# Lightning attention and a bilinear FFN on one core: the first FFN step of four token groups as seven block products

## The chip, the cores and the metric

The kernel runs on one core of a Trainium2 chip. The metric is the device time of one execution in microseconds (us). A core has five engines with queues of their own: TensorE (PE; its weight loads are listed apart as PEld), VectorE (DVE), ScalarE (ACT), GpSimd (POOL) and SyncE (SP), which here issues nearly all DMAs. Each engine takes its instructions in the order in which the program gives them, so an instruction that waits holds up all that stands behind it on that engine.

## What is computed

Attention with decay in blocks, then a bilinear FFN, all in float32 outside and bf16 inside the matrix products:

```
q, k, v: (4, 8, 768, 64)      # batch, heads, sequence, head size
for each block of the sequence:
    intra = ((qb @ kb.T) * Dmask) @ vb
    inter = (qb * lam_pow) @ kv_state
    out   = intra + inter
    kv_state = lam_block * kv_state + (kb * rev_pow).T @ vb

x = out as (3072 tokens, 512)
a = x @ w_a                   # 512 x 1536
b = x @ w_b                   # 512 x 1536
y = (a * b) @ w_out           # 1536 x 512
```

The result y is 3072 x 512 in float32.

## The kernel before

The tokens are cut into 24 units of 128 (a unit is 128 positions of one batch entry, all heads). `GROUPS` = (4, 1, 2, 4, 4, 4, 4, 1) joins units into eight groups; group 3 holds units 7 to 10, group 4 holds 11 to 14, and so on, and the last group is unit 23 alone. The FFN of a group runs while the attention of units further on is worked in between its matmuls. Group 0 also brings in the weights: they come as float32 through the 12 staging buffers of `wst_pool` and are cast to bf16 into `wa_sb`, `wb_sb` and `wo_sb`.

The FFN of a later group (`ffn`, L518) has two stages. In the first, each of 12 column blocks f of the weights takes four matmuls for `a_ps` and four for `b_ps` (`half`, L465): weights 128x128 stand still, up to 512 tokens of xT move. ScalarE copies `a_ps` to `a_sb` (L477), VectorE multiplies `a_sb` with `b_ps` into `ab` (L495). In the second, the output stage, each unit t of the group takes 12 matmuls into `op` (L515), ScalarE copies the result to `o_sb` (L510), and SP stores it. The outputs of the first three groups are kept in `wst` buffers (L505) and stored in group 3.

What is done between the matmuls is written out by hand in `PLAN`: for each group a list of (slot, piece, unit). `hook(slot)` issues the pieces of a slot; slots 0 to 11 follow the column blocks f, slots 12 and up the half units of the output stage (12 + 2t after the first six matmuls of unit t, 13 + 2t after its store). In group 0 slots 12 to 35 follow pairs of output matmuls. The pieces:

- P (also split into PK and PV): `prep_k` (L298) multiplies k and q by powers of lam (L276; POOL, for units 4 and 5 k on VectorE), from unit 7 on issues a DMA transpose on SP (L304) to make `qkT`; `prep_v` (L309) casts v to `vb` (L295; POOL up to unit 6, then VectorE) and calls `pump` (L188), which issues the loads of units further on. How far on is set by `LOOKAHEAD`: three units while fewer than nine are prepared, then two, with exceptions at 9 and 10. The loads have four buffers per tensor.
- T: transposes on PE for units 4 to 6 (L318), with a copy by ScalarE (L320).
- S: scores on PE (L332) and their masks on VectorE (L349). V: the state update on PE (L396) and its copy on VectorE (L429). O, O2, Q: `pieces_O` (L442): inter and intra matmuls (L366), ScalarE's copies to xT (L389), and in Q the scores and masks of two more units before and after.
- C: a cast of `wo_sb`. W: a store of a kept output.

PSUM has seven banks of this kernel in rotation (`ps_bank`, L110), which a piece can hold, and one for the state. An allocation takes the next bank that is not held; the first writer of the new tile waits for the last reader of the old one.

Of the kernel before, what the change touches and what calls it, by code (L numbers as in the profile page):

```python
# [16 lines left out]
F32 = mybir.dt.float32  # L17
BF16 = mybir.dt.bfloat16
# [4 lines left out]
def _bc(ap, dims):  # L23
# [4 lines left out]
GROUPS = (4, 1, 2, 4, 4, 4, 4, 1)  # L28
# [11 lines left out]

PLAN = {
    0: [(0, "V", 3), (8, "C", 0), (9, "C", 1), (15, "C", 2), (18, "C", 3), (23, "PK", 4),
        (26, "C", 4), (26, "T", 4), (29, "C", 5), (29, "S", 4), (30, "PV", 4), (33, "O", 4),
# [4 lines left out]
        (9, "S", 7), (9, "S", 8), (6, "PK", 10), (10, "V", 8), (11, "PV", 10),  # L50
        (12, "Q", (7, 8, 9, 10)), (12, "P", 11), (13, "V", 9), (14, "P", 12),
        (14, "O2", (9, 10))],
    3: [(6, "S", 11), (6, "S", 12)],
}
for _g, _u in ((3, 11), (4, 15), (5, 19)):
    PLAN.setdefault(_g, []).extend(
        [(1, "P", _u + 2), (3, "P", _u + 3), (6 if _g == 3 else 4, "V", _u),
         (9 if _g == 3 else 7, "Q", (_u, _u + 1, _u + 2, _u + 3)), (10, "P", _u + 4),
         (12, "P", _u + 5), (13, "V", _u + 2), (16, "Q", (_u + 2, _u + 3, _u + 4, _u + 5))])
PLAN[3] += [(_s, "W", None) for _s in range(12, 19)]  # L60
PLAN[5] = [(_s, _n, (21, 22, 23) if _us == (21, 22, 23, 24) else _us)
           for _s, _n, _us in PLAN[5] if _us != 24]
PLAN[6] = [(4, "O", 23)]


@with_exitstack
def kernel(
# [11 lines left out]
    nc = tc.nc  # L79
    B, H, S, D = q.shape  # L80
# [3 lines left out]
    d_model, d_ff = moe_w_a.shape  # L84
# [4 lines left out]
    FC = d_ff // 128  # L89
# [3 lines left out]
    wst_pool = ctx.enter_context(tc.tile_pool(name="wst", bufs=W_BUFS))  # L93
    ld_pool = ctx.enter_context(tc.tile_pool(name="ld", bufs=4))
# [3 lines left out]
    xT_pool = ctx.enter_context(tc.tile_pool(name="xT", bufs=2))  # L98
    a_pool = ctx.enter_context(tc.tile_pool(name="a", bufs=5))
    ab_pool = ctx.enter_context(tc.tile_pool(name="ab", bufs=2))  # L100
    o_pool = ctx.enter_context(tc.tile_pool(name="o", bufs=4))
    ps_pool = ctx.enter_context(tc.tile_pool(name="ps", bufs=1, space=PSUM))
    kvps_pool = ctx.enter_context(tc.tile_pool(name="kvps", bufs=1, space=PSUM))

# [5 lines left out]
    def ps_bank(name, shape, dt, hold=False, ffn=False, at=None):  # L110
        i = bank["next"] if at is None else at
        while i in bank["held"] or (ffn and i == bank["ffn"]):
            i = (i + 1) % 7
        if ffn:
            bank["ffn"] = i
        bank["next"] = (i + 1) % 7
        if hold:
            bank["held"].add(i)
        return ps_pool.tile(shape, dt, name=name, tag=f"ps{i}")
# [6 lines left out]

    def load_x(w, u):
        b, nb = divmod(u, NB)
        t = ld_pool.tile([128, H, D], F32, name=w + "f", tag=w + "f")
        nc.sync.dma_start(out=t, in_={"q": qr, "k": kr, "v": vr}[w][b, nb])  # L130
        raw[u, w] = t

# [176 lines left out]
    def prep_v(u):  # L309
        make_vb(u, "pool" if u < n0 + 3 else "dve")  # L310
        pump()
# [70 lines left out]
    def evac_o(us, b, eng="act"):  # L382
        xT, col = xTs[us[0]]
        n = len(us)
        o = U[us[0]]["o"][b]
        src = _bc(o, [o.ap[0], [2 * BLK, 2], [1, n * BLK]])
        dst = xT[:, 2 * b:2 * b + 2, col:col + n * BLK]
        if eng == "act":
            nc.scalar.copy(dst, src)  # L389
        else:  # L390
            nc.vector.tensor_copy(dst, src)
# [48 lines left out]
    xTs = {}  # L440

    def pieces_O(us, nxt=()):  # L442
        kqs = [score_banks() for u in nxt]
        o_banks(us)
        for u, kq in zip(nxt, kqs):
            scores(u, kq)
        for u in us:
            inter(u)
        for b in range(2):
            for u in us:  # L450
                intra(u, b)
            evac_o(us, b)
        beside = len(us) == 2 and us[0] >= n0 + 5
        if beside:
            kv_beside(us[1])
        for u, kq in zip(nxt, kqs):
            masks(u, kq)
        if beside and us[1] % NB < NB - 1:
            kv_copy(us[1], kv["ps"])
# [34 lines left out]
        ps = half(wb_sb, f, xT, "b_ps", 0, gt)  # L494
        nc.vector.tensor_mul(ab[:, f, :gt], a_sb[:, :gt], ps[:, :gt])  # L495

    kept = []

    def store_kept():
        row, o_sb = kept.pop(0)  # L500
# [1 line left out]

    def store(row, op, lo, hi, queue=None):
        if row < g_u0[KEEP_GROUPS]:
            o_sb = wst_pool.tile([128, 1024], F32, name="o_kept", tag="wst")[:, :d_model]  # L505
            nc.scalar.copy(o_sb, op)
            kept.append((row, o_sb))
            return
        o_sb = o_pool.tile([128, d_model], F32, name="o_sb", tag="osb")
        nc.scalar.copy(o_sb[:, lo:hi], op[:, lo:hi])  # L510
        (queue or nc.sync).dma_start(out=out_r[row][:, lo:hi], in_=o_sb[:, lo:hi])

    def out_mms(op, ab, t, fs, lo=0, hi=d_model):
        for f in fs:
            nc.tensor.matmul(op[:, lo:hi], lhsT=ab[:, f, t * 128:(t + 1) * 128],  # L515
                             rhs=wo_sb[:, f, lo:hi], start=(f == 0), stop=(f == FC - 1))

    def ffn(u0, n, xT, hook, first, last):  # L518
        gt = n * BLK
        ab = ab_pool.tile([128, FC, 512], BF16, name="ab", tag="ab")  # L520
        if first:
            for i, cs in enumerate(W_STEPS):
                nxt = W_STEPS[i + 1] if i + 1 < len(W_STEPS) else ()
                fs = range(w_off[cs[0]] // 128, w_off[cs[-1] + 1] // 128)
                a_sbs = a_parts(fs[:2], xT, gt) if i == 0 else []
                a_sbs += [a_part(f, xT, gt) for f in fs[len(a_sbs):]]
                if i == 0:
                    cast_w("b", cs[1], "act")
                else:
                    for c in nxt:  # L530
                        cast_w("a", c, "dve")
                for n_f, (f, a_sb) in enumerate(zip(fs, a_sbs)):
                    b_part(f, xT, gt, a_sb, ab)
                    hook(f)
                    if i == 0 and n_f == 1:
                        cast_w("a", nxt[0], "dve")
                for c in nxt:
                    cast_w("b", c, "act")
            ops = [ps_bank("op", [128, d_model], F32, hold=True) for _ in range(n)]
            slot = FC  # L540
            for c in range(FC // 2):
                for t in range(n):
                    out_mms(ops[t], ab, t, range(2 * c, 2 * c + 2))
                    if c == FC // 2 - 1:
                        store(u0 + t, ops[t], 0, d_model)
                    hook(slot)
                    slot += 1
            bank["held"].clear()
            return
        for f in range(FC):  # L550
            a_sb = a_part(f, xT, gt)
            b_part(f, xT, gt, a_sb, ab)
            hook(f)
        for t in range(n):
            op = ps_bank("op", [128, d_model], F32, ffn=True)
            if last and t == n - 1:
                for lo, hi in ((0, 256), (256, 384), (384, 512)):
                    if lo:
                        op = ps_bank("op", [128, d_model], F32, ffn=True)
                    out_mms(op, ab, t, range(FC), lo, hi)  # L560
                    store(u0 + t, op, lo, hi, nc.scalar if hi == d_model else None)
                return
            out_mms(op, ab, t, range(FC // 2))
            hook(FC + 2 * t)
            out_mms(op, ab, t, range(FC // 2, FC))
            store(u0 + t, op, 0, d_model)
            hook(FC + 2 * t + 1)


    gx = {}  # L570
# [134 lines left out]
    for g, n in enumerate(GROUPS):  # L705
        if g + 1 < len(GROUPS):
            new_xT(g + 1)
        plan = {}
        for slot, name, us in PLAN.get(g, ()):
            plan.setdefault(slot, []).append((name, us))  # L710

        def hook(slot, plan=plan):
            for name, us in plan.get(slot, ()):
                if name == "C":
                    cast_w("o", us, "dve")
                elif name == "PK":
                    prep_k(us)
                elif name == "PV":
                    prep_v(us)
                elif name == "P":  # L720
                    prep_k(us)
                    prep_v(us)
                elif name == "W":
                    store_kept()
                elif name == "T":
                    piece_T(us)
                elif name == "S":
                    piece_S(us)
# [12 lines left out]
_INS = ['q', 'k', 'v', 'lam', 'moe_w_a', 'moe_w_b', 'moe_w_out']  # L741
# [26 lines left out]
```

## Time and profile before

Three runs gave 231.8, 232.08 and 233.04 us, median 232.08. The profiled execution spans 230.2 us from the first to the last instruction, at a granted TensorE clock of 0.999. By group, each row the busy time in a stretch of that execution:

| stretch, us | what | PE | DVE | ACT | POOL | DMA, GB/s |
|---|---|---|---|---|---|---|
| 51.3 to 62.2 | group 1 | 10.85 | 6.11 | 6.48 | 6.86 | 197 |
| 62.2 to 82.3 | group 2 | 19.73 | 14.45 | 7.68 | 8.17 | 197 |
| 82.3 to 117.5 | group 3 | 34.79 | 20.93 | 11.52 | 12.62 | 235 |
| 117.5 to 152.1 | group 4 | 34.39 | 17.37 | 11.51 | 8.53 | 165 |
| 152.1 to 187.0 | group 5 | 34.58 | 16.05 | 11.51 | 2.22 | 76 |
| 187.0 to 218.8 | group 6 | 31.64 | 8.26 | 10.02 | 0.00 | 34 |

A row of a group listing reads: line, engine, operation, output and input tiles, shapes and number; after the first bar the busy time in all (us) and the mean of one (ns); after the second the idle time of the engine just ahead of these instructions and what ended it. A row of a timeline reads: start, length (us), engine, line, operation, tiles, number of instructions merged, and in brackets the idle time before it. On PE the end of a matmul is modelled, so consecutive ones overlap in the print; the distance between starts is what counts.

### The profile page before, as it was taken

What the parts mean: (1) busy time and instruction counts of PE and PEld (TensorE: products, weight loads), DVE (VectorE), ACT (ScalarE), POOL (GpSimd) and SP (SyncE); (2) the same over time, 40 slices, a digit from 0 to 9 for tenths busy, and PEclk for the clock granted to TensorE, in tenths of its full rate; (3) what the DMA queues carried; (4) which work ended last, traced back from release to release, by engine and by line L of the source; (5) the groups of instructions that cost most, each with busy time, mean ns of one, the idle gap of its engine ahead of it and who ended that gap; (6) DMA issues with size and microseconds to landing.
All of it is one profiled execution on the core that took longest, in us unless ns stands there. A gap on an engine that the chain in (4) does not pass through costs nothing.

```text
span 230.2 us, 4630 instructions
## 1 busy us (share of the span) xinstructions
PE 221.4 (96%) x1816; PEld 121.0 (53%) x1839; DVE 118.2 (51%) x205; ACT 88.8 (39%) x172; POOL 49.9 (22%) x65
## 2 busy tenths in 40 slices
PE   7699999999999999999999999999999999999994
PEld 2475444459688544454544454544454544444493
DVE  0994865736488845876416574426574313341050
ACT  2686563056433243242233342233342233432261
POOL 6061000228351436333302433002100000000000
PEclk9999999999999999999999999999999999999999
DMA  4999999999999999999979995249200220000211
GB/s 130 317 277 347 363 387 293 303 217 196 202 211 182 215 186 231 233 195 200 350 222 217 157 235 89 94 116 205 48 0 0 94 91 0 4 0 31 106 48 47
DMA packets 97542, 39.37 MB, mean 171 GB/s; under 512 B 85488, under 2 KB 92016, under 8 KB 97520
## 3 DMA queue, kind: packets, MB, share of 16 engines
q1 hardware_dynamic: 97232, 39.00, 75.2%
q8 instruction: 14, 0.23, 0.4%
q10 hardware_dynamic: 288, 0.07, 0.1%
q14 instruction: 8, 0.07, 0.1%
HBM read 28.32 MB, written 6.29 MB: 150 GB/s over the span
## 4 chain that ended last, share of the span: by engine, by line
PE 92%; DMA 3%; SPq 1%; issue 1%; ACT 1%; DVE 0%
PE a_ps L468 27%; PE b_ps L468 27%; PE op L515 27%; PE o_ps L366 5%; DMA k<-in_k_dram 3%; PE kq L332 3%; PE kvd L396 2%; SPq L224 1%; PE tps L318 1%; PE kq L633 1%; PE kv L396 0%; PE tk L597 0%; DVE scratch L587 0%; PE kvd L418 0%; ACT scratch L608 0%
## 5 line engine op out<-in xcount | busy, mean ns | idle before, releaser
L495 DVE TENSOR_TENSOR ab<-a_sb,b_ps 128x512 bf16<-128x512 bf16 (+2 forms) x96 | 52.2, 552 | 75.5 <-PE b_ps L468 55.1
L468 PE MATMUL a_ps<-xT,wa_sb 128*128 128x512 bf16 (+2 forms) x384 | 76.3, 322 | 0.6 <-ACT xT L389 0.3
L468 PE MATMUL b_ps<-xT,wb_sb 128*128 128x512 bf16 (+2 forms) x381 | 76.6, 325 | 0.2
L477 ACT CAST a_sb<-a_ps 128x512 bf16<-128x512 f32 (+2 forms) x96 | 45.2, 481 | 62.4 <-PE a_ps L468 60.0
L515 PE MATMUL op<-wo_sb,ab 128*128 128x512 bf16 (+2 forms) x300 | 63.9, 362 | 1.0 <-issue 0.6
L468 PEld LDWEIGHTS <-wb_sb 128*128 128x128 bf16 x384 | 34.5, 98 | 28.7 <-ACT wb_sb L169 0.2
L468 PEld LDWEIGHTS <-wa_sb 128*128 128x128 bf16 x392 | 34.4, 98 | 28.3 <-DVE wa_sb L171 0.5
L515 PEld LDWEIGHTS <-ab 128*128 128x128 bf16 x312 | 28.7, 98 | 29.9
L349 DVE TENSOR_TENSOR m<-kq,lotri 128x512 bf16<-128x512 f32 x47 | 29.3, 683 | 15.8 <-PE kq L332 15.7
L276 POOL TENSOR_TENSOR qk<-kf,lp_k 128x512 bf16<-128x512 f32 x18 | 18.8, 1042 | 73.9 <-DMA kf<-in_k_dram 60.7
L276 POOL TENSOR_TENSOR qk<-qf,lp_q 128x512 bf16<-128x512 f32 x20 | 21.9, 1097 | 22.6 <-DMA qf<-in_q_dram 22.6
L510 ACT COPY o_sb<-op 128x512 f32<-128x512 f32 (+2 forms) x19 | 10.3, 541 | 34.0 <-PE op L515 34.0
L389 ACT CAST xT<-o_ps 128x512 bf16<-128x512 f32 (+1 forms) x24 | 12.1, 555 | 17.5 <-PE o_ps L366 17.4
L429 DVE TENSOR_TENSOR st<-kvd,bdiag 128x512 bf16<-128x512 f32 x18 | 12.3, 683 | 3.2 <-PE kvd L396 3.2
L295 DVE CAST vb<-vf 128x512 bf16<-128x512 f32 x17 | 11.6, 682 | 3.8 <-DMA vf<-in_v_dram 3.7
L366 PE MATMUL o_ps<-m,vb 128*64 128x128 bf16 x192 | 8.0, 222 | 0.0
L208 PE MATMUL idle<-idle_sb 128*128 128x512 bf16 (+2 forms) x23 | 6.5, 411 | 1.3 <-DVE idle_sb L203 1.3
L295 POOL CAST vb<-vf 128x512 bf16<-128x512 f32 x7 | 4.3, 611 | 13.7 <-DMA vf<-in_v_dram 13.7
L320 ACT COPY qkT<-tps 128x1024 bf16<-128x1024 bf16 x3 | 3.0, 1012 | 10.6 <-PE tps L318 10.6
L332 PEld LDWEIGHTS <-qkT 64*128 64x128 bf16 x160 | 4.5, 94 | 4.2 <-issue 3.2
L332 PE MATMUL kq<-qkT 64*128 64x128 bf16 x160 | 6.6, 218 | 0.1
L366 PEld LDWEIGHTS <-vb 128*64 128x64 bf16 x192 | 5.8, 109 | 1.3
(58 smaller groups left out, 81.0 us busy)
## 6 DMA issues: line engine op xcount, KB each, us to landing
vf<-in_v_dram SPq DMA_DIRECT2D x24, 256.0 KB, 5.0
qf<-in_q_dram SPq DMA_DIRECT2D x20, 256.0 KB, 4.2
kf<-in_k_dram SPq DMA_DIRECT2D x20, 256.0 KB, 4.6
out_dram<-o_sb SPq DMA_DIRECT2D x16, 256.0 KB, 2.0
wst<-in_moe_w_a_dram SPq DMA_DIRECT2D x6, 512.0 KB, 8.6
wst<-in_moe_w_b_dram SPq DMA_DIRECT2D x6, 512.0 KB, 8.9
wst<-in_moe_w_out_dram SPq DMA_DIRECT2D x6, 512.0 KB, 10.6
out_dram<-o_kept SPq DMA_DIRECT2D x7, 256.0 KB, 4.0
```

Source lines behind the costliest of these rows:

```text
L276: eng_of(eng).tensor_mul(dst.rearrange("p (c b) d -> p b c d", b=2), x[:].rearrange("p (b c) d -> p b c d", b=2), lp.rearrange("p (b c) o ...
L295: eng_of(eng).tensor_copy(vb, vf)
L332: nc.tensor.matmul(kq[i][:, hp, :], lhsT=d["kT"][p, hp, :], rhs=d["qT"][p, hp, :], start=True, stop=True, skip_group_check=True)
L349: nc.vector.tensor_mul(m, kq[i], lotri_bc)
L366: nc.tensor.matmul(U[u]["o"][b][p, c // 2, :], start=new[b, h % 2], stop=True, skip_group_check=True, **ops)
L389: nc.scalar.copy(dst, src)
L429: nc.vector.tensor_mul(st[:].rearrange("p c b d -> p c (b d)"), ps[:].rearrange("p c b d -> p c (b d)"), bdiag_bc)
L468: nc.tensor.matmul(ps[:, lo:hi], lhsT=w_sb[:, s, f * 128:(f + 1) * 128], rhs=xT[:, s, lo:hi], start=(s == 0), stop=(s == KS - 1), skip_gro ...
L477: nc.scalar.copy(a_sb[:, :gt], ps[:, :gt])
L495: nc.vector.tensor_mul(ab[:, f, :gt], a_sb[:, :gt], ps[:, :gt])
L510: nc.scalar.copy(o_sb[:, lo:hi], op[:, lo:hi])
L515: nc.tensor.matmul(op[:, lo:hi], lhsT=ab[:, f, t * 128:(t + 1) * 128], rhs=wo_sb[:, f, lo:hi], start=(f == 0), stop=(f == FC - 1))
```

## The change

Groups 3 to 6 (`S_GROUPS`) get `ffn_seven` in place of `ffn`. Their four units are cut into two halves of 256 tokens and the 512 rows of the weights into two halves of 256. With x11, x12 the two row halves of the first 256 tokens, x21, x22 of the second, and a1, a2, b1, b2 the halves of two column blocks of w_a and w_b, the four sums of products that `a` and `b` need (eight products) are made of seven:

- weight sums t0 = b1 - a1, t1 = b2 - t0, t2 = b2 - b1, t3 = a2 - t1 (`w_sums`, once for each pair of column blocks, six sets kept in `wst` buffers to the end: four made by POOL in groups 0 and 1, two by VectorE in group 2)
- token sums s0 = x22 + x21, s1 = s0 - x11, s2 = x11 - x21, s3 = x12 - s1 (`sums`, on VectorE, once a group, after the group's last attention output)
- products 1: a1 x11, 2: a2 x12, 3: b2 s3, 4: t3 x22, 5: t0 s0, 6: t1 s1, 7: t2 s2

Products 1, 6, 7 and 4 add up in one bank (`m_q`), 5 and 3 in another (`m_r`), 2 has a third. ScalarE copies `m_q` after product 1 (s1) and after 6 (u2), `m_r` after 5 (s5) and the bank of 2 (s2). POOL adds s1 and s2 to c11 and multiplies c11 with c12 into the first half of `ab`; VectorE makes c12 = u2 + `m_r`, c22 = s5 + `m_q`, and the second half of `ab` from c22 and the full `m_q`. A product is two column blocks times two row blocks, four matmuls of 256 columns. The steps of pair i start at 7i, interleaved with those of i - 1.

In these groups PLAN keeps preparing units in the first stage (slots 1, 3, 9), and puts V, Q, O2 and S at slots 11 to 19. Group 6 puts O of unit 23 at slot 13. The q and k load buffers go from four to three, those of `o_sb` from four to three, kept outputs share a `wst` buffer in pairs.

```diff
+S_GROUPS = (3, 4, 5, 6)
-    3: [(6, "S", 11), (6, "S", 12)],
+    3: [(11, "S", 11), (11, "S", 12)],
+    6: [(13, "O", 23)],
 for _g, _u in ((3, 11), (4, 15), (5, 19)):
-        [(1, "P", _u + 2), (3, "P", _u + 3), (6 if _g == 3 else 4, "V", _u),
-         (9 if _g == 3 else 7, "Q", (_u, _u + 1, _u + 2, _u + 3)), (10, "P", _u + 4),
-         (12, "P", _u + 5), (13, "V", _u + 2), (16, "Q", (_u + 2, _u + 3, _u + 4, _u + 5))])
+        [(1, "P", _u + 2), (3, "P", _u + 3), (9, "P", _u + 4), (11, "V", _u),
+         (12, "Q", (_u, _u + 1, _u + 2, _u + 3)), (14, "V", _u + 2),
+         (16, "O2", (_u + 2, _u + 3)), (18, "S", _u + 4)])
+    if _u + 5 < 24:
+        PLAN[_g] += [(12, "P", _u + 5), (19, "S", _u + 5)]
-PLAN[6] = [(4, "O", 23)]
+PLAN[0] += [(_s, "TW", (_f, "pool")) for _s, _f in ((31, 0), (34, 1))]
+PLAN[1] += [(_s, "TW", (_f, "pool")) for _s, _f in ((8, 2), (11, 3))]
+PLAN[2] += [(_s, "TW", (_f, "dve")) for _s, _f in ((3, 4), (5, 5))]
...
-    o_pool = ctx.enter_context(tc.tile_pool(name="o", bufs=4))
+    o_pool = ctx.enter_context(tc.tile_pool(name="o", bufs=3))
+    sn_pool = ctx.enter_context(tc.tile_pool(name="sn", bufs=1))
...
-        t = ld_pool.tile([128, H, D], F32, name=w + "f", tag=w + "f")
+        t = ld_pool.tile([128, H, D], F32, name=w + "f", tag=w + "f", bufs=4 if w == "v" else 3)
...
             evac_o(us, b)
+        sums(us[-1])
...
+    def w_sums(i, eng):
+        t = wst_pool.tile([128, 4, 2, 256], BF16, name="tw", tag="wst")
+        e = nc.gpsimd if eng == "pool" else nc.vector
+        e.tensor_sub(t[:, 0], b1, a1)
+        e.tensor_sub(t[:, 1], b2, t[:, 0])
+        e.tensor_sub(t[:, 2], b2, b1)
+        e.tensor_sub(t[:, 3], a2, t[:, 1])
...
+        def snap(name, ps, bufs):
+            t = sn_pool.tile([128, 2, 256], F32, name=name, tag=name, bufs=bufs)
+            nc.scalar.copy(t, ps)
+            return t
...
+            if n == 1:
+                product(i, d["q"], w_of(wa_sb, 0, i), x11, True)
+                d["s1"] = snap("s1", d["q"], 2)
+            elif n == 5:
+                product(i, d["r"], t_of(0, i), st[:, 0], True)
+                d["s5"] = snap("s5", d["r"], 2)
+            elif n == 2:
+                product(i, p, w_of(wa_sb, 2, i), x12, True)
+                s2 = snap("s2", p, 1)
+                nc.gpsimd.tensor_add(d["c11"], d["s1"], s2)
+            elif n == 6:
+                product(i, d["q"], t_of(1, i), st[:, 1], False)
+                d["u2"] = snap("u2", d["q"], 1)
+            elif n == 3:
+                product(i, d["r"], w_of(wb_sb, 2, i), st[:, 3], False)
+                nc.vector.tensor_add(c12, d["u2"], d["r"])
+                nc.gpsimd.tensor_mul(ab[:, 2 * i:2 * i + 2, 0:256], d["c11"], c12)
+            elif n == 7:
+                product(i, d["q"], t_of(2, i), st[:, 2], False)
+                nc.vector.tensor_add(d["c22"], d["s5"], d["q"])
+            else:
+                product(i, d["q"], t_of(3, i), x22, False)
+                nc.vector.tensor_mul(ab[:, 2 * i:2 * i + 2, 256:512], d["c22"], d["q"])
...
+            for off, n in ((0, 1), (2, 5), (3, 2), (4, 6), (6, 3), (8, 7), (12, 4)):
+                at[7 * i + off] = (i, n)
...
+            if s % 7 == 1 and s < 42:
+                hook(2 * (s // 7))
+            if s % 7 == 4 and s < 35:
+                hook(2 * (s // 7) + 1)
+        hook(FC - 1)
+        op = ps_bank("op", [128, d_model], F32, ffn=True)
+        out_mms(op, ab, 0, range(FC // 2))
+        step(*at[end])
+        hook(FC)
+        out_mms(op, ab, 0, range(FC // 2, FC))
+        store(u0, op, 0, d_model)
```

The rest of the output stage is that of `ffn`.

## The prediction, made before the changed kernel was run

> **What bounds the kernel now.** I read the page first: engine shares, DMA row, chain of waits.
>
> ```profile
> span 230.2 us, 4630 instructions
> PE 221.4 (96%) x1816; PEld 121.0 (53%) x1839; DVE 118.2 (51%) x205; ACT 88.8 (39%) x172; POOL 49.9 (22%) x65
> ...
> DMA  4999999999999999999979995249200220000211
> ...
> PE 92%; DMA 3%; SPq 1%; issue 1%; ACT 1%; DVE 0%
> ```
>
> TensorE (PE) carries 92% of the chain, so a microsecond of matmul saved is a microsecond of time, as long as PE is never made to wait. The other engines are half idle; the DMA row is full up to about slice 23, that is to 132 us. What a matmul costs is read in the timeline, PE alone, from one block of four to the next:
>
> ```profile
> 62.18 0.60 PE L468 MATMUL a_ps<-xT,wa_sb 128*128 128x256 bf16 x4
> 62.61 0.60 PE L468 MATMUL b_ps<-xT,wb_sb 128*128 128x256 bf16 x4
> ...
> 117.46 1.03 PE L468 MATMUL a_ps<-xT,wa_sb 128*128 128x512 bf16 x4
> 118.32 1.03 PE L468 MATMUL b_ps<-xT,wb_sb 128*128 128x512 bf16 x4
> ```
>
> Blocks start 0.437 us apart at 256 columns (over 62.18 to 66.33, less the 0.22 of one kvd block) and 0.864 at 512: half the columns cost 0.506 of the time, weight loads included. A consumer starts 0.1 us after the printed end (a 256 block from 62.18: ScalarE at 62.86), so 0.70 after a block's start. Next the early part, where the change puts new GpSimd (POOL) work. POOL's timeline, then the points where PE and SP need it:
>
> ```profile
> 45.09 0.61 POOL L295 CAST vb<-vf 128x512 bf16<-128x512 f32 x1 [3.76 <-DMA vf<-in_v_dram]
> 46.74 1.04 POOL L276 TENSOR_TENSOR qk<-qf,lp_q 128x512 bf16<-128x512 f32 x1 [1.04 <-DMA qf<-in_q_dram]
> ...
> 55.48 1.04 POOL L276 TENSOR_TENSOR qk<-kf,lp_k 128x512 bf16<-128x512 f32 x1 [0.32 <-DMA kf<-in_k_dram]
> ```
> ```profile
> 52.89 0.61 PE L318 MATMUL tps<-ident,qk 128*128 128x128 bf16 x8
> ...
> 71.45 0.62 PE L332 MATMUL kq<-qkT 64*128 64x128 bf16 x16
> ```
> ```profile
> 61.14 1.92 SPq L304 DMA_TRANSPOSE qkT<-qk  x1
> ...
> 65.38 5.91 SPq L304 DMA_TRANSPOSE qkT<-qk  x3
> ```
>
> At 52.89 PE transposes unit 5, whose scaled q left POOL at 47.8: 5 us spare. At 71.45 it takes the scores of units 7 and 8, whose DMA transposes were issued from 61.1: a landing takes 4.3 us (median of the tile view for qkT), so spare is small. The groups' price of one operation:
>
> ```profile
> L276 POOL TENSOR_TENSOR qk<-kf,lp_k 128x512 bf16<-128x512 f32 x18 | 18.8, 1042 | 73.9 <-DMA kf<-in_k_dram 60.7 <-PE b_ps L468 3.6 <-issue 3.3
> L295 POOL CAST vb<-vf 128x512 bf16<-128x512 f32 x7 | 4.3, 611 | 13.7 <-DMA vf<-in_v_dram 13.7
> L347 POOL TENSOR_TENSOR m<-scratch,lotri 128x512 bf16<-128x512 bf16 x1 | 1.2, 1158 | 0.0
> ```
>
> POOL's idle time is mostly waiting for loads: its order and the load queue feed each other.
>
> [...] The trace shows vb casts of 0.42 us alone and 1.05 beside POOL, and POOL products of 1.22 for 1.04. [...]
>
> **The change part by part.**
>
> *Matmuls.* A group of four units has 24 blocks of 512 in the first step, 24 x 0.864 = 20.74 us; now 42 blocks of 256, 42 x 0.437 = 18.37. Gain 2.36 a group, 9.46 for four. Second step and attention matmuls are the same in number: before, a group takes 34.7 us (117.5 to 152.1), of which 20.74 + 10.37 + some 3.6 of attention.
>
> *Inside a period of seven products (3.06 us).* ScalarE has four copies instead of two: 4 x 0.49 (start to start, back to back) = 1.96 us. VectorE has three operations reading PSUM, 3 x 0.60 to 0.69, at most 2.06. Each return to an accumulating bank has four product slots, 1.75 us, for 0.70 + 0.59 to 0.69 (+0.1 queue) = 1.39: 0.36 spare. These cost nothing while nothing is late. POOL has c11 and the first product of ab, 2 x 1.05, but preparing a unit puts 2.08 more in its queue. With units at slots 1 and 3, in the first two periods, POOL is 2.2 us behind; `s2` has one buffer, so ScalarE's copy of it waits for the c11 of the period before, and the copies behind it on ScalarE (u2, which PE's seventh product waits for) wait too. By hand, from the group's start: c11 of period 0 on POOL 2.65 to 3.7, a unit to 5.8, product of ab to 6.9, c11 of period 1 to 7.9, a unit to 10.0, product to 11.0, c11 of period 2 to 12.1. The s2 copy of period 3 could start at 3 x 3.06 + 2.06 = 11.24 and gets its buffer at 12.2: 0.96 late, 0.36 covered, 0.6 of PE per group that prepares units. Last, the fourth score bank at slot 12 is the last product's bank, freed by a multiply that starts 0.70 after the delayed product: 0.7 of PE; in group 3, where two pairs of masks are put ahead of it on VectorE, 1.5. `sums` [...] lie in the 5 us between slot 16 and the next group: nothing.
>
> *Weight sums.* 16 operations on POOL, 8 on VectorE. [...] On POOL they stand in its queue ahead of the preparation of units 5 and 7. I take 1.05 each (bounds 1.00, the spacing of f32 pairs, and 1.16, the bf16 row). Group 0's two sets run from 45.70 (after vb of unit 4) to 54.1; scaled q of unit 5 is done at 55.1: PE waits 2.2 at 52.89, with all of group 1 queued behind these transposes. Then vb5, unit 6, vb6 (3.2), sets 2 and 3 (8.4), unit 7 (2.0): 68.7, where before it was 57.5. Then SP, in its order: transpose 7 to 70.7, loads of unit 10 (2.2, as at 63.12 to 65.28) to 72.9, transpose 8 to 74.9, landing 77.2. PE is at those scores at 71.45 + 2.2 = 73.65: 3.5 more, lag 5.7. k of unit 10 lands at 75.9 (4.6 median), its transpose at 82.3; PE wants it at 75.44 + 5.7 + 0.3: 0.9, lag 6.6. v of unit 11 lands at 86.2 and its cast holds VectorE ahead of the state of unit 9 (87.3), wanted at 79.83 + 6.6: 0.9, lag 7.5. Group 3 starts at 82.27 + 7.5 = 89.8, while k of units 13 and 14 lands at 94.5 and 98.7, in the middle of POOL's c11 chain, which now stands behind these loads: 0.4 + 1.2 = 1.6 of PE instead of 0.6. This is the step that decides: POOL ran ahead of PE before, and now cannot.
>
> *Moved attention.* No new instruction. Its DMAs (transposes, loads) come at slots 1, 3, 9, 12; from group 4 on a load is issued at least 12 us before its use, so POOL's 12 to 17 us waits on kf vanish; they hid behind PE anyway: no gain. Three load buffers in place of four and three output buffers: each is released by work that is done before; nothing. On SP the stores of a group's rows now stand behind the transpose of the unit prepared at slot 12, which waits for POOL some 2 us after the last product of ab; the first row is only ready 3 us after it, so nothing, and up to 1 us for one store if POOL is late, which no one waits for with three buffers.
>
> *Sum.* Early lag +7.5; group 3: -2.36 + 1.6 + 1.5 = +0.7; groups 4 and 5: -2.36 + 1.3 = -1.05 each; group 6 (one unit's output, no preparation): -2.36. Together +3.8 on a span of 230.2: 234.0. The median shown, 232.08, is 1.9 above the profiled span; so 235.9 us.
>
> **The rivals.** *Not slower: POOL's sums fit.* The lag at group 3 grows by 16 us per us of a POOL sum. Break-even needs a lag 3.8 smaller, a sum of about 0.8 us; below 0.4 nothing is late and the time is 232.1 - 9.46 + 1.3 x 2 + 1.5 + 0.6 = 227.3. For it: casts of the same size take 0.61, and POOL is 22% busy. Against it: both two-input rows are over 1.0. *No change:* loads land faster in a DMA queue that the delay has emptied (3.1 was the shortest transpose, 4.1 the shortest kf load): 1.2 + 0.5 + 1.2 less: about 233. *POOL becomes the bound in all groups:* at the contended 1.23 us, 18 operations of a first step are 22.1 against PE's 18.37; c11 must keep pace, so of 3.7 over some 2.1 falls on PE (0.6 counted): +1.5 in three groups, and 16 x 0.18 = 2.9 in the early chain: 243. For it: vb casts and sums now lie beside a POOL that never rests. [...] No throttling shows before (clock 0.999 of 1)[...].
>
> **How the numbers follow.** Forecast 0.56, at 235.9 (233.2 to 239: sums at 1.00 to 1.16 give -0.8 and +1.8, faster landings up to -2.9, steady waits -1 to +2). POOL fits, 227.3: 0.12. About unchanged, 231 to 233: 0.12. POOL bounds, 239 to 245: 0.20. A measurement of this kernel can tell 0.5%, 1.2 us, from no change: faster 0.13, same 0.12, slower 0.75. Range 230.0 to 242.5: it leaves out the first rival and the upper third of the last.
>
> **What would show it.** A PE gap of 2 us before the transposes of unit 5 behind POOL, one of 3 to 4 before the scores of unit 8 behind qkT, group 3 starting near 90; products 0.437 apart; small ScalarE and VectorE waits in groups 4 to 6, which take near 33.6, 33.6 and, where before 31.8 passed, 29.4. Wrong if POOL sums take under 0.8, if unit 7's preparation is not behind them, or if groups 4 and 5 don't get shorter.

## The result, and the profile after

Four runs of the changed kernel gave 245.79 to 247.3 us, median 246.3, against 232.26 for four runs of the kernel before: a ratio of 1.060, interval 1.056 to 1.064. It is slower by 14.0 us; 3.8 were predicted. The page of the kernel after, top and chain:

```profile
span 244.6 us, 5389 instructions
...
PE 219.7 (90%) x2108; PEld 151.2 (62%) x2127; DVE 145.1 (59%) x253; ACT 112.5 (46%) x220; POOL 126.1 (52%) x129
...
PEclk9999999997999999979999999999999999999999
...
PE 56%; DMA 17%; POOL 8%; issue 6%; SPq 5%; DVE 5%; ACT 2%; POOLq 0%; DVEq 0%; ACTq 0%
```

TensorE's share of the chain fell from 92% to 56%: in the early part of the run the chain now goes through loads, SP, POOL and VectorE. PE's granted clock, 9 tenths or more in every slice before, falls to 7 in two slices. By group, from the first matmul of one group to that of the next:

| length, us | group 1 | group 2 | group 3 | group 4 | group 5 | group 6 |
|---|---|---|---|---|---|---|
| before | 10.9 | 20.1 | 35.2 | 34.7 | 34.7 | 31.8 |
| after | 15.5 | 24.5 | 41.3 | 35.1 | 34.9 | 29.7 |
| difference | +4.6 | +4.4 | +6.1 | +0.4 | +0.2 | -2.1 |

With 0.6 before group 1 these make the 14.4 us between the two spans. That 0.6 is chance: `e3_s2_two` and `e10_v_on_pool`, below, have the same program up to there and start group 1 at 51.1, the kernel before at 51.3. Two stretches of the kernel after, group 1 and group 6 (length, then busy time and number of instructions of PE, PEld, DVE, ACT, POOL, then granted clock, DMA share, GB/s):

```profile
51.95:67.43 15.48, 12.31 (x168) 9.98 (x168) 6.57 (x18) 6.66 (x18) 15.25 (x16) 0.89 0.78 146
...
203.30:232.97 29.67, 29.57 (x232) 21.39 (x232) 11.83 (x19) 15.62 (x30) 14.64 (x12) 1.00 0.10 37
```

In group 1 POOL is busy for 15.25 of 15.48 us, where it was 6.86 of 10.85. In group 6, where nothing is prepared, PE never stops, and the whole gain of the seven products is there.

**Group 1.** POOL's timeline, then PE's:

```profile
46.10 1.16 POOL L509 TENSOR_TENSOR tw<-wb_sb,wa_sb 128x512 bf16<-128x512 bf16 x1
...
54.58 1.15 POOL L512 TENSOR_TENSOR tw<-wa_sb,tw 128x512 bf16<-128x512 bf16 x1
55.69 1.05 POOL L281 TENSOR_TENSOR qk<-qf,lp_q 128x512 bf16<-128x512 f32 x1
```
```profile
56.79 1.03 PE L323 MATMUL tps<-ident,qk 128*128 128x128 bf16 x8 [3.12 <-POOL qk L281]
57.62 0.63 PE L474 MATMUL a_ps<-xT,wa_sb 128*128 128x128 bf16 x4
58.05 0.63 PE L474 MATMUL b_ps<-xT,wb_sb 128*128 128x128 bf16 x4
...
59.71 0.39 PE L474 MATMUL b_ps<-xT,wb_sb 128*128 128x128 bf16 x4
59.93 0.39 PE L474 MATMUL a_ps<-xT,wa_sb 128*128 128x128 bf16 x4
```

Eight weight sums, seven of 1.15 to 1.16 us and one of 1.60, stand ahead of the scaled q of unit 5, and PE waits 3.12 for it. Afterwards its blocks start 0.43 us apart (57.62 to 58.05), later 0.22 (59.71 to 59.93): the granted clock was 0.50 from 56.23 to 59.65, and 1.00 again behind it. That cost 1.4: five blocks from 57.62 took 2.09 in place of 1.11, and the transposes 0.83 to the next start where the next set took 0.45. 3.1 + 1.4 make 4.5 of group 1's +4.6. (In the traces of `e3_s2_two` and `e10_v_on_pool`, with the same program up to there, this wait is 3.67 and 4.46: one trace of this part is good to about 1 us.)

**Group 2.** VectorE's timeline, one of its weight sums beside POOL and one without it, and what PE makes of it:

```profile
73.62 1.26 DVE L511 TENSOR_TENSOR tw<-wb_sb 128x512 bf16<-128x512 bf16 x1
...
77.77 0.42 DVE L511 TENSOR_TENSOR tw<-wb_sb 128x512 bf16<-128x512 bf16 x1
```
```profile
76.45 0.60 PE L474 MATMUL a_ps<-xT,wa_sb 128*128 128x256 bf16 x4 [1.42 <-DVE ab L501]
...
89.73 0.31 PE L371 MATMUL o_ps<-qkT,st 64*64 64x128 bf16 x8 [1.18 <-DVE st L434]
```

The same operation took 1.26 us at 73.62, while POOL made scaled products (1.22 us each, the last to 75.78), and 0.42 at 77.77, where POOL was idle (75.78 to 78.41). The multiplies into `ab` stand behind these sums, so banks come free late. PE waits 1.42, then 0.56 and 0.85 behind VectorE, and 1.18 for the state of unit 9: 4.0 of the +4.4.

**Group 3.** PE's timeline, then VectorE's:

```profile
93.71 0.61 PE L541 MATMUL m_r<-xs,tw 128*128 128x256 bf16 x4 [1.14 <-DVE xs L521]
...
99.31 0.60 PE L541 MATMUL m_q<-xT,tw 128*128 128x256 bf16 x4 [1.43 <-DVE c L587]
...
103.24 0.60 PE L541 MATMUL m_r<-xs,tw 128*128 128x256 bf16 x4 [2.03 <-DVE ab L590]
103.67 0.71 PE L541 MATMUL m_p<-xT,wa_sb 128*128 128x256 bf16 x4
104.18 1.06 PE L541 MATMUL m_q<-xs,tw 128*128 128x256 bf16 x4
105.03 1.06 PE L541 MATMUL m_q<-xT,tw 128*128 128x256 bf16 x4
```
```profile
91.95 0.52 DVE L300 CAST vb<-vf 128x512 bf16<-128x512 f32 x1 [2.28 <-DMA vf<-in_v_dram]
92.39 1.26 DVE L521 TENSOR_TENSOR xs<-xT 128x512 bf16<-128x512 bf16 x1
...
96.85 1.21 DVE L300 CAST vb<-vf 128x512 bf16<-128x512 f32 x1 [1.47 <-DMA vf<-in_v_dram]
97.98 0.68 DVE L581 TENSOR_TENSOR c<-u,m_r 128x512 f32<-128x512 f32 x1
98.58 0.67 DVE L587 TENSOR_TENSOR c<-s,m_q 128x512 f32<-128x512 f32 x1
...
101.54 1.05 DVE L300 CAST vb<-vf 128x512 bf16<-128x512 f32 x1 [2.29 <-DMA vf<-in_v_dram]
102.51 0.68 DVE L590 TENSOR_TENSOR ab<-c,m_q 128x512 bf16<-128x512 f32 x1
```

Read the two together: each of PE's three waits ends at a VectorE operation that stood behind a cast of v, and each cast had itself waited for a load. The page names `xs`, `c` and `ab`; the cause is one row higher in VectorE's queue. After the third wait the products start 0.85 us apart (104.18 to 105.03) instead of 0.44, at a granted clock of 0.50 from 104.02 to 107.43: five from 103.67 took 3.85 us in place of 2.19.

The kernel before has the same casts at the same slots, and one is late there too. Its VectorE timeline, at the preparation in slot 3:

```profile
91.24 1.32 DVE L295 CAST vb<-vf 128x512 bf16<-128x512 f32 x1 [1.27 <-DMA vf<-in_v_dram]
92.48 1.27 DVE L495 TENSOR_TENSOR ab<-a_sb,b_ps 128x512 bf16<-128x512 bf16 x2
```

Two multiplies into `ab` stand behind it, and yet nothing holds PE for more than 0.16 anywhere in that group. What changed, as far as these lines show, is the slack behind such a cast. Before, each block of four matmuls takes the next of the seven banks; now PE comes back to the same bank after four products, which the prediction itself put at 0.36 us of spare time.

**Groups 4 and 5.** The same pattern stands in both. One row of ScalarE's timeline, one of PE's, and POOL's two groups from the page:

```profile
141.41 0.59 ACT L555 COPY s<-m_p 128x512 f32<-128x512 f32 x1 [0.67 <-POOL c L574]
```
```profile
146.88 0.60 PE L541 MATMUL m_q<-xs,tw 128*128 128x256 bf16 x4 [1.13 <-ACT u L555]
```
```profile
L574 POOL TENSOR_TENSOR c<-s,s 128x512 bf16<-128x512 f32 x24 | 30.5, 1272 | 44.9 <-ACT s L555 44.8
...
L583 POOL TENSOR_TENSOR ab<-c,c 128x512 bf16<-128x512 bf16 x24 | 28.2, 1174 | 4.4 <-DVE c L581 3.8
```

ScalarE's copy s2 waits for its only buffer, which c11 on POOL holds, and u2 behind it holds PE's seventh product: 0.23 and 1.13 us in each group.

### The profile page after: what moved, and what is told of

Its sections match the earlier page's. It is cut to its first block, busy times and chain, and to the rows that moved or that the text cites. A ratio compares the mean times of both kernels' runs of the same rounds, so it can differ in the third digit from the quotient of the medians.

```text
span 244.6 us, 5389 instructions
## 1 busy us (share of the span) xinstructions
PE 219.7 (90%) x2108; PEld 151.2 (62%) x2127; DVE 145.1 (59%) x253; ACT 112.5 (46%) x220; POOL 126.1 (52%) x129
## 4 chain that ended last, share of the span: by engine, by line
PE 56%; DMA 17%; POOL 8%; issue 6%; SPq 5%; DVE 5%; ACT 2%; POOLq 0%; DVEq 0%; ACTq 0%
PE op L642 18%; PE m_q L541 14%; PE m_r L541 7%; DMA qf<-in_q_dram 4%; PE a_ps L474 4%; PE b_ps L474 4%; DMA wst<-in_moe_w_a_dram 3%; PE m_p L541 3%; DMA wst<-in_moe_w_b_dram 3%; SPq L135 3%; POOL qk L281 3%; DMA kf<-in_k_dram 2%; PE o_ps L371 2%; DMA q<-in_q_dram 2%; DMA vf<-in_v_dram 2%
## 5 line engine op out<-in xcount | busy, mean ns | idle before, releaser
L574 POOL TENSOR_TENSOR c<-s,s 128x512 bf16<-128x512 f32 x24 | 30.5, 1272 | 44.9 <-ACT s L555 44.8
L541 PEld LDWEIGHTS <-tw 128*128 128x128 bf16 x384 | 37.8, 99 | 14.9 <-issue 7.2
L501 DVE TENSOR_TENSOR ab<-a_sb,b_ps 128x128 bf16<-128x128 bf16 (+2 forms) x48 | 19.3, 417 | 29.4 <-ACT a_sb L483 21.7
L354 DVE TENSOR_TENSOR m<-kq,lotri 128x512 bf16<-128x512 f32 x47 | 29.5, 684 | 5.2 <-PE kq L337 4.9
L541 PE MATMUL m_q<-xs,tw 128*128 128x256 bf16 x192 | 29.2, 275 | 2.7 <-ACT u L555 2.7
L583 POOL TENSOR_TENSOR ab<-c,c 128x512 bf16<-128x512 bf16 x24 | 28.2, 1174 | 4.4 <-DVE c L581 3.8
L474 PE MATMUL a_ps<-xT,wa_sb 128*128 128x128 bf16 (+2 forms) x198 | 28.3, 272 | 2.3 <-DVE ab L501 1.4
L474 PE MATMUL b_ps<-xT,wb_sb 128*128 128x128 bf16 (+2 forms) x192 | 28.1, 276 | 0.1
L590 DVE TENSOR_TENSOR ab<-c,m_q 128x512 bf16<-128x512 f32 x24 | 16.5, 687 | 19.3 <-PE m_q L541 19.3
L483 ACT CAST a_sb<-a_ps 128x128 bf16<-128x128 f32 (+2 forms) x48 | 17.4, 376 | 18.3 <-PE a_ps L474 15.4
L394 ACT CAST xT<-o_ps 128x512 bf16<-128x512 f32 (+1 forms) x24 | 12.2, 556 | 26.6 <-PE o_ps L371 26.5
L474 PEld LDWEIGHTS <-wb_sb 128*128 128x128 bf16 x192 | 16.1, 100 | 6.0 <-ACT wb_sb L174 0.2
L555 ACT COPY s<-m_r 128x512 f32<-128x512 f32 x24 | 14.1, 588 | 10.8 <-PE m_r L541 10.8
L555 ACT COPY s<-m_q 128x512 f32<-128x512 f32 x24 | 14.2, 590 | 10.6 <-PE m_q L541 10.2
## 6 DMA issues: line engine op xcount, KB each, us to landing
wst<-in_moe_w_out_dram SPq DMA_DIRECT2D x6, 512.0 KB, 10.5
```

What stands on the lines that cost most here:

```text
L354: nc.vector.tensor_mul(m, kq[i], lotri_bc)
L474: nc.tensor.matmul(ps[:, lo:hi], lhsT=w_sb[:, s, f * 128:(f + 1) * 128], rhs=xT[:, s, lo:hi], start=(s == 0), stop=(s == KS - 1), skip_gro ...
L483: nc.scalar.copy(a_sb[:, :gt], ps[:, :gt])
L541: nc.tensor.matmul(ps[:, f, :], lhsT=w(k, f), rhs=x[:, k, :], start=(first and f == 0 and k == 0), stop=True, skip_group_check=True)
L555: nc.scalar.copy(t, ps)
L574: nc.gpsimd.tensor_add(d["c11"], d["s1"], s2)
```

## The experiments

The group lengths of all runs, from the same reading of PE's timeline (start of group 3, then lengths; ratios to the kernel before with their intervals). The lengths are those of one traced execution, the medians those of all; the traces of e7, e8 and e9 are of executions 1.4, 2.6 and 0.8 us longer than their medians:

| run | median | ratio | start of 3 | 3 | 4 | 5 | 6 |
|---|---|---|---|---|---|---|---|
| before | 232.3 | | 82.3 | 35.2 | 34.7 | 34.7 | 31.8 |
| after | 246.3 | 1.060 (1.056 to 1.064) | 92.0 | 41.3 | 35.1 | 34.9 | 29.7 |
| e1_no_weight_sums | 234.2 | 1.012 (1.002 to 1.023) | 82.2 | 38.9 | 35.1 | 34.9 | 29.7 |
| e2_sums_between | 241.3 | 1.040 (1.034 to 1.045) | 82.3 | 45.7 | 35.1 | 34.9 | 29.7 |
| e3_s2_two | 241.7 | 1.041 (1.035 to 1.047) | 91.6 | 39.6 | 33.5 | 33.3 | 29.7 |
| e4_plan_only | 233.4 | 1.006 (1.004 to 1.009) | 82.0 | 36.5 | 35.0 | 34.8 | 31.8 |
| e5_no_sums_late_units | 233.8 | 1.007 (1.003 to 1.011) | 82.4 | 38.1 | 35.1 | 34.9 | 29.7 |
| e6_all_moved | 231.8 | 0.998 (0.996 to 1.000) | 82.9 | 39.0 | 33.5 | 33.3 | 29.7 |
| e7_c11_dve | 231.7 | 0.998 (0.996 to 0.999) | 84.4 | 37.3 | 34.2 | 33.7 | 29.6 |
| e8_c11_dve_v_pool | 228.6 | 0.986 (0.980 to 0.992) | 82.9 | 38.6 | 34.2 | 33.1 | 29.6 |
| e9_group3_order | 230.8 | 0.989 (0.986 to 0.993) | 82.8 | 35.7 | 37.6 | 33.1 | 29.6 |
| e10_v_on_pool | 245.6 | 1.057 (1.054 to 1.061) | 92.8 | 38.0 | 36.0 | 35.8 | 29.7 |
| e11_stores_g4 | 227.5 | 0.982 (0.977 to 0.987) | 83.6 | 34.7 | 33.3 | 33.1 | 29.5 |
| e12_stores_early_g3 | 227.9 | 0.980 (0.977 to 0.984) | 83.9 | 34.7 | 33.2 | 33.1 | 29.5 |

**The weight sums taken out.** `w_sums` isn't called, and `t_of` returns a slice of `wb_sb`.

```diff
-PLAN[0] += [(_s, "TW", (_f, "pool")) for _s, _f in ((31, 0), (34, 1))]
-PLAN[1] += [(_s, "TW", (_f, "pool")) for _s, _f in ((8, 2), (11, 3))]
-PLAN[2] += [(_s, "TW", (_f, "dve")) for _s, _f in ((3, 4), (5, 5))]
```

> The 24 weight sums are left out; the products read rows of w_b unsummed, so the output is not the reference's. Theory A (the sums stand in GpSimd's and VectorE's queues ahead of the preparation of units 5 to 9, and through the load chain all of the excess of groups 1 to 3 comes from them): group 1 starts near 51.5, group 2 near 62.5, group 3 near 83, group 3 takes about 35 to 36 us instead of 41.3, span about 231, time about 233. Rival B (group 3's excess comes from seven products being worked while loads still arrive, whoever delayed them): groups 1 and 2 as before, but group 3 still takes 39 to 41 us; span about 235 to 236, time about 237.

The span fell from 244.6 to 232.4: the sums account for 12.2 us, 9.8 of them before group 3. Group 3 stays 3.7 above before, though nothing is late when it starts. Two of its waits are as in the kernel after:

```profile
88.79 0.60 PE L538 MATMUL m_q<-xT,wb_sb 128*128 128x256 bf16 x4 [1.43 <-DVE c L584]
92.72 0.60 PE L538 MATMUL m_r<-xs,wb_sb 128*128 128x256 bf16 x4 [2.02 <-DVE ab L587]
```

So group 3 loses on its own account too: groups 1 and 2 came out as in the kernel before, and group 3, at 38.9, lies next to rival B's 39 to 41. Nor do the loads come later here: the casts of units 13 and 14 start at 86.79 and 91.59, where the kernel before has them at 86.60 and 91.24. So the smaller number of load buffers isn't what delays them.

**The sums cut into single operations between the preparations.** 16 on POOL in slots 1 to 14 of group 2, eight on VectorE in slots 2 to 8 of group 3.

```diff
-    def w_sums(i, eng):
+    def w_sums(n, eng):
+        i, j = divmod(n, 4)
...
+        x, y = ((b1, a1), (b2, t[:, 0]), (b2, b1), (a2, t[:, 1]))[j]
+        e.tensor_sub(t[:, j], x, y)
```

> All 24 sums are made, but one by one: 16 on GpSimd in group 2, behind the preparation of units 8, 9, 10, 11 and 12, in gaps in which it waited for loads before, the last 8 on VectorE in group 3. Theory A (order in the queue, not the amount of work): within 2 us of the kernel without sums, span 231 to 234. Rival B (it is the amount: 17.8 us of GpSimd work have no room before group 3): span 238 or more, as the delay only moves from group 1 to groups 2 and 3.

Groups 1 and 2 are whole again, and group 3 loses 10.5 in all. The sums of tokens now take 1.26 to 1.37 each beside POOL, and PE waits 1.4 and 2.0 for them, 2.6 behind the product into `ab` and 1.2 for ScalarE's u2. The work was moved, not hidden, as rival B has it (span 239.3).

**Two buffers for s2**, in bf16, so that both fit.

```diff
-                s2 = snap("s2", p, 1)
+                s2 = snap("s2", p, 2, BF16)
```

> s2 gets two buffers (in bf16, so that they fit). Theory A (the single buffer of s2 makes ScalarE's copies wait for GpSimd's c11, and PE for u2): the PE waits for ACT u of 0.23 and 1.13 in group 4 and again in group 5 vanish, groups 4 and 5 take about 33.7 us each instead of 35.1 and 34.9, time about 2.7 us less, near 243.6. Rival (GpSimd is simply over its capacity in the first step, and the wait moves to ab or to c11 itself): groups 4 and 5 stay within 0.5 of 35.

The waits for u2 are gone, and groups 4 and 5 are 1.6 shorter each: that one buffer was the cost there, as theory A has it. The time fell by 4.7 and not by 2.7: in this trace group 3 is shorter too, since behind its waits of 1.31 and 1.91 the products kept their 0.44 from start to start (98.97 to 99.40, 102.79 to 103.22).

**The moved attention alone**: the kernel before, with eight products, and of the change only these lines of `PLAN`.

```diff
-    3: [(6, "S", 11), (6, "S", 12)],
+    3: [(11, "S", 11), (11, "S", 12)],
+    6: [(13, "O", 23)],
...
+        [(1, "P", _u + 2), (3, "P", _u + 3), (9, "P", _u + 4), (11, "V", _u),
+         (12, "Q", (_u, _u + 1, _u + 2, _u + 3)), (14, "V", _u + 2),
+         (16, "O2", (_u + 2, _u + 3)), (18, "S", _u + 4)])
```

> The kernel before with only the moved attention (the changed PLAN of groups 3 to 6), all products as eight. Theory A (the move itself costs nothing, as forecast): 232 us within 0.7. Rival (gathered in the output stage the attention pieces wait for their own masks and copies): 1.5 us or more slower, seen as PE waits in pieces_O and longer output stages of groups 3 to 5.

Neither expectation holds: the median is 1.3 above that of the kernel before. The move costs 1.3 in group 3 and 0.4 in groups 4 and 5 together; the part before group 3 happened to be 0.3 shorter. Its timeline shows 0.5 of this as waits (for masks of VectorE); the remainder isn't assigned.

**Units 13 to 15 prepared later in group 3**, at slots 4, 7 and 11, without weight sums (as in the first experiment, `t_of` returns a slice of `wb_sb`).

```diff
+PLAN[3] = [({13: 4, 14: 7, 15: 11}.get(_us, _s) if _n == "P" else _s, _n, _us)
+           for _s, _n, _us in PLAN[3]]
```

> As the run without weight sums (raw rows of w_b, the output is not the reference's), and in group 3 units 13, 14 and 15 are prepared at slots 4, 7 and 11 instead of 1, 3 and 9. Theory (what is left of group 3's excess, 38.9 us against 35.3 before, is c11 on GpSimd and c12, c22 and the product of ab on VectorE queued behind preparations whose k and v loads have not landed): group 3 takes 34 to 35.5 us, the waits of PE for DVE c and DVE ab vanish, time about 230. Rival (group 3 is long because GpSimd has too much work in the first stage, whenever the loads land): 38 us or more as before, and waits for ACT u instead.

The waits for c22 and for `ab` inside the first stage vanish, but group 3 gains only 0.8: 1.3 us more of waits for u2 (4.0 in all), 1.5 at the inter matmuls for an `ab`, and 1.0 for the sums of tokens took their place. A miss of theory; length and waits are those of the rival: one late engine removed shows the next.

**The whole computation with these edits joined**: two s2 buffers, the later units, twelve weight sums on POOL between the preparations of group 2, twelve on VectorE at the ends of groups 0 and 1. Then c11 on VectorE straight from the bank of product 2, so that s2 and its copy fall away; then the casts of v from unit 13 on POOL.

```diff
-                s2 = snap("s2", p, 2, BF16)
-                nc.gpsimd.tensor_add(d["c11"], d["s1"], s2)
+                nc.vector.tensor_add(d["c11"], d["s1"], p)
...
-        make_vb(u, "pool" if u < n0 + 3 else "dve")
+        make_vb(u, "pool" if u < n0 + 3 or u > 12 else "dve")
```

> The whole computation: two buffers for s2 (bf16); units 13 to 15 later as in the run before; the 24 sums so that nothing waits behind them: 12 on GpSimd in group 2 between the preparations of units 8 to 11, 12 on VectorE in groups 0 and 1 while GpSimd is idle. Theory (the change lost by the order in the queues and one buffer): groups 1 and 2 as before, groups 3 to 5 near 34, 33.5, 33.3, group 6 29.7: span 224 to 225.5, time 226 to 227.5, faster than before by 2 to 2.6%. Rival ([...]the sums cost 1.2 us each wherever they lie): over 229.

> As the run before, but c11 is made on VectorE from s1 and the product's bank, without the copy s2 and without GpSimd. Theory A (GpSimd's 1.27 us for c11 still delays ab and the units): 0.5 to 1.5 us faster than the run before. Rival (VectorE now has four operations of up to 0.69 in 3.06 us and the casts of v besides, and is late for c22): 1 to 4 us slower, with PE waiting for DVE c22.

> As the run before, with the casts of v of units 13 and up on GpSimd, so that no operation on VectorE in groups 3 to 6 waits for a load. Theory A (VectorE must be kept free of loads and of work): 0.5 us or more faster than the run with c11 on VectorE alone. Rival (the casts fitted into VectorE's gaps anyway): within 0.5 us.

The first is level with the kernel before, a miss (226 to 227.5 was expected). The second gains nothing over the first, where 0.5 to 1.5 was expected, nor does it lose what its rival names. The third is 3.1 faster than the second, as expected, and 1.4% faster than the kernel before. The 24 sums, placed like this, delay group 3 by 0.6 in the first of these runs, against 9.7 in the kernel after. Group 3 stays the long one, at 37 to 39: PE still waits 1.6 to 2.2 for the sums of tokens.

**The order of group 3**: scores of units 11 and 12 at slots 8 and 10, unit 12 prepared after the last output pieces of group 2 (its cast no longer ahead of the sums of tokens), unit 15 at slot 12.

```diff
-        (12, "Q", (7, 8, 9, 10)), (12, "P", 11), (13, "V", 9), (14, "P", 12),
-        (14, "O2", (9, 10))],
-    3: [(11, "S", 11), (11, "S", 12)],
+        (12, "Q", (7, 8, 9, 10)), (12, "P", 11), (13, "V", 9),
+        (14, "O2", (9, 10)), (14, "P", 12)],
+    3: [(8, "S", 11), (10, "S", 12)],
```

> As the run with c11 on VectorE and v casts on GpSimd, and in group 3 the three places changed at which PE still waited for VectorE: unit 12's cast of v behind the token sums instead of ahead of them, the scores and masks of units 11 and 12 at slots 8 and 10 instead of both at 11, unit 15 prepared at slot 12. Theory (group 3's last excess is order on VectorE plus the clock that drops behind such waits): group 3 takes 33.5 to 35 us instead of 38.6, no matmuls at the lower clock in it, time 224 to 226. Rival (a first stage with seven products can't take the masks of two units besides): group 3 stays above 37, with new waits for DVE c22 or for a bank.

Group 3 falls to 35.7, close to the 33.5 to 35 expected, but group 4 rises by 3.4, and the time, 230.8, is no gain over the run before (228.6). ScalarE's, PE's and SP's timelines:

```profile
121.40 0.59 ACT L637 COPY o_sb<-op 128x512 f32<-128x512 f32 x1 [5.58 <-DMA out_dram<-o_sb]
```
```profile
122.04 0.68 PE L542 MATMUL m_p<-xT,wa_sb 128*128 128x256 bf16 x4 [2.50 <-ACT o_sb L637]
122.53 1.04 PE L542 MATMUL m_q<-xs,tw 128*128 128x256 bf16 x4
```
```profile
114.38 0.92 SPq L136 DMA_DIRECT2D vf<-in_v_dram  x1
115.34 1.23 SPq L626 DMA_DIRECT2D out_dram<-o_kept  x1
116.67 0.38 SPq L638 DMA_DIRECT2D out_dram<-o_sb  x1
117.10 1.06 SPq L626 DMA_DIRECT2D out_dram<-o_kept  x2
118.26 0.79 SPq L638 DMA_DIRECT2D out_dram<-o_sb  x1
```

The first row of group 3, copied at 108.7, is stored only at 116.67: transposes and loads of units 15 and 16 and a kept store are ahead of it on SP. With three `o_sb` buffers the fourth copy waits, and ScalarE's snapshots with it. Behind the wait of 2.50 the products started 0.85 apart (123.37 to 124.22), as they did at a clock of 0.50 in the kernel after, and the mean clock of this execution was 0.993: five products from 122.04 took 3.85 in place of 2.19, so 1.7 of the 3.4 are put down to the clock.

**The casts of v from unit 12 on POOL, alone, in the kernel after.**

```diff
-        make_vb(u, "pool" if u < n0 + 3 else "dve")
+        make_vb(u, "pool" if u < n0 + 3 or u > 11 else "dve")
```

> The changed kernel with one edit: v of units 12 and up is cast on GpSimd instead of VectorE, so in group 3 no VectorE operation waits for a load. Theory (the waits of 1.4 and 2.0 us of PE for DVE c22 and DVE ab in group 3, and the lower clock behind them, come from VectorE's casts waiting for v): both vanish, group 3 takes 37 to 38.5 us instead of 41.3, but groups 4 and 5 grow by 0.3 to 1 each, as GpSimd has 0.61 more per unit; time 242 to 244. Rival (GpSimd's wait for k of the same units holds c11 as long, and PE waits for u instead): group 3 within 1 us of 41.3, time 246 or more.

The waits for c22 and for `ab` in group 3's first stage are gone, and the group is 3.3 shorter (41.3 to 38.0): 3.5 of waits and 1.7 of halved clock are gone, 1.9 of waits for u2 came in. The run with later units ended the same two waits with the casts still on VectorE. Together they show the cause: the casts of v, placed where their loads had not landed. Groups 4 and 5 pay 0.9 each on POOL (waits for u2 in all 6.5, after 2.7), and this run's wait for unit 5 was 4.5 in place of 3.1, so the total hardly moves (242 to 244 was expected).

**The stores out of the way**: `e9_group3_order` with the kept stores in group 4, unit 16 prepared at slot 15 and four `o_sb` buffers; then the same with the kept stores at the start of group 3.

```diff
-PLAN[3] += [(_s, "W", None) for _s in range(12, 19)]
+PLAN[4] += [(_s, "W", None) for _s in range(2, 9)]
...
-    o_pool = ctx.enter_context(tc.tile_pool(name="o", bufs=3))
+    o_pool = ctx.enter_context(tc.tile_pool(name="o", bufs=4))
```

> The whole computation: the run e9_group3_order with three things moved. The seven kept stores of groups 0 to 2 are issued in slots 2 to 8 of group 4 in place of slots 12 to 18 of group 3, unit 16 is prepared in slot 15 of group 3 in place of 12, and there are four output buffers in place of three. Theory A (ScalarE's copy in group 4 waited because the stores of group 3 stood on SP behind kept stores, transposes and loads, so that the output buffers came free late): group 3 stays at 35.5 to 36.5 us, group 4 falls from 37.6 to 33.3 to 34.5, span about 225.5 to 227, time about 227. Rival B (the transfers themselves were late, whatever SP's order, because the DMA engines are full there): the wait for an output store stays in one of the two groups, group 3 and 4 together stay above 72, time 230 or more.

> As e11_stores_g4, but the seven kept stores are issued in slots 0 to 6 of group 3, beside the loads of v that VectorE and GpSimd's casts wait for. Theory A (order on SP decides): the stores of group 3 are no longer behind them, so group 4 is 33.3 to 34.5 as in e11; group 3 may lose up to 1 us to later loads. Rival B (transfers are full): group 3 rises by 2 us or more, to 38 or above. Time 227 to 228.5 under A, 230 or more under B.

Both give the same lengths, so it doesn't matter whether the kept stores stand at the start of group 3 or in group 4. Groups 3 and 4 together take 67.9, so theory A holds in both. Which of the three edits ended the wait for an output buffer wasn't separated, and of the 4.3 that group 4 gains over the run before, 1.7 are the clock. The first of the two, page and windows of groups 3 and 4:

```profile
PE 214.2 (95%) x2108; PEld 148.7 (66%) x2127; DVE 157.3 (70%) x270; ACT 102.5 (45%) x196; POOL 98.0 (43%) x112
...
PEclk9999999999999999999999999999999999999999
```
```profile
83.64:118.31 34.67, 33.52 (x334) 23.92 (x336) 27.71 (x47) 15.07 (x27) 20.05 (x22) 1.00 0.97 182
118.31:151.56 33.25, 32.59 (x322) 23.71 (x321) 24.62 (x40) 14.95 (x27) 17.18 (x18) 1.00 1.17 231
```

PE is 95% busy, the granted clock is 9 tenths or more in every slice (1.00 in both groups), and the kernel is 1.8% faster than before (interval 1.3 to 2.3). Of the 9.5 us that the products save, 4.9 are left in the span (230.2 to 225.3).

## Why the prediction was wrong

*Right.* Its direction; the price of a product (0.44 from start to start) and with it group 6 (29.4 predicted, 29.7 measured); the place where POOL's weight sums first hurt; unit 7's preparation ending up behind them (at 71.0; 68.7 predicted).

*The step that failed most: group 3, "-2.36 + 1.6 + 1.5 = +0.7".* It was +6.1, so 5.4 of the 10.6 us that the forecast was short in the span. The 1.6 was worked out from POOL's queue, the 1.5 from the last score bank; in the trace PE doesn't wait for u2 in group 3 at all, and waits 0.6 near the score banks. VectorE's queue wasn't followed: its casts of v are issued by the preparations in slots 1 and 3, and stand ahead of the block sums that give PE its banks back. The text put the state update of unit 9 behind the cast of v of unit 11, and did not ask the same question one group on. "These cost nothing while nothing is late" was the sentence that stopped the working. The cast-on-POOL run shows this cause: 3.3 us net. The sums of tokens, called "nothing", were held by such a cast as well: 1.1. The halved clock adds 1.7, and the moved attention, also called "nothing", 1.3. The parts overlap and aren't to be added: the group is 2.4 longer with the weight sums than without them, and 1.7 of that is the halved clock. The run without them had the same two waits (1.43 and 2.02), and behind both its products started 0.43 to 0.44 apart. That groups 4 and 5 didn't get shorter is the sign of being wrong that the prediction itself names.

*The early lag, 7.5 predicted and 9.7 measured.* At unit 5 the wait was 3.12 for 2.2: the sum was at the upper of the two bounds, 1.16 for 1.05, times eight. The halved clock (1.4) is no term of the sum. The wait of 3.5 before the scores of unit 8 didn't come; PE lost its time earlier in that group, since the weight sums on VectorE in group 2, for which the lag has no term, cost 2.8 of PE: every `ab` of group 2 goes through VectorE. The last wait, for the state of unit 9, was 1.18 for 0.9. The 0.6 before group 1 is chance.

*Groups 4 and 5, -1.05 predicted and +0.4 and +0.2 measured.* The mechanism, one s2 buffer and POOL behind by a preparation, was right, and the size was not: 1.36 us for 0.6. Two terms of the sum were off. POOL's chain was slower, c11 at 1.27 and not 1.05, the product of `ab` at 1.17: c11 of period 2 ended 12.4 us after the group's start (144.46 + 1.27 - 133.28) where 12.1 was worked out. And the s2 copy of period 3 was wanted earlier than the 11.24 of the text: its product starts at 143.41, so with the 0.70 of the text it could start at 10.8. The text gave all periods seven products, but the first of a group has five, since it has no pair before it. A wait of 0.23 one period earlier wasn't seen. Against this, the wait at the score bank was 0.4 for 0.7. The products saved 2.1 and not 2.36, as group 6 shows, and the moved attention costs 0.1 to 0.3. With two buffers the groups are 33.5 and 33.3, where the prediction's terms without the s2 wait give 33.0; all but some 0.2 of each is in these terms.

*The rivals.* "POOL bounds in all groups", 243, came nearest in time and not in mechanism: the loss fell before group 4, 15.8 us by its start. That it lies nearest is luck.

## What to carry to other kernels

A sum saved on the bound engine is paid on the others' queues: before the matmuls are counted, write down for each helper engine what stands ahead of each operation that frees a bank, and mark those that wait for a load or a store. Then compare the delay with the slack: how many products pass before TensorE comes back to that bank. Such an operation belongs on an engine, or at a point in the order, where nothing that TensorE waits for is behind it. Take the dearer bound for a new sum on VectorE that runs beside a busy GpSimd (here 1.26 us for 0.42), and follow SP's order for stores as for loads.

## What the runs showed of the hardware

- The clock. In the kernel after the granted clock was 0.50 in three stretches, from 56.23 to 59.65, from 104.02 to 107.43 and from 243.97 to the end, and 1.00 elsewhere; in the kernel before it was 0.50 only from 229.78 to the end. The first two stretches lasted 3.41 us each, and the full-speed stretches between them 44.37 and 136.53 us, 13 and 40 times as much. In the 3.41 us ahead of the four PE was idle for 2.56, 2.03, 2.8 and 3.0 us (with matmul ends as the profile models them). Of all the other stretches of 3.41 us, counted on from these, none in the two traces had PE idle for more than 1.43.
- The longest single wait doesn't tell whether the clock falls. In `e1_no_weight_sums` the products behind a wait of 2.02 started 0.43 us apart (92.72 to 93.15), in `e6_all_moved` those behind one of 1.64 0.44 (85.16 to 85.60), both as at full clock. In `e6_all_moved` again, at a mean clock of 0.990, 11 output matmuls behind a wait of 1.31 took 4.06 us (109.14 to 113.20) where 11 took 2.47 later (117.37 to 119.84). What decides isn't shown.
- The same program can keep the clock or lose it: `e1_no_weight_sums` has a mean clock of 1.0 in two executions and 0.992 in the third, which is 2.4 us longer; `e6_all_moved` keeps 1.0 in 6 of 20.
- A bf16 sum of two SBUF tiles on VectorE took 0.42 us while POOL was idle (77.77 in the kernel after) and 1.26 beside POOL's products (73.62), a factor of three.
- POOL's time for 128x512: 1.04 us for a scaled product with a broadcast factor (70.01 in the kernel after), 1.15 to 1.16 for a sum of two bf16 tiles (seven of the eight from 46.10 on), 1.27 for c11 of two f32 tiles (mean of 24).
